# Dividing after the value product: where softmax's reciprocals are multiplied in

## The chip, the cores and the metric

The kernel runs on one core of a Trainium2 chip. The core has five engines that take their instructions in order, each from a queue of its own: TensorE (PE, with its weight loads shown apart as PEld), VectorE (DVE), ScalarE (ACT), GpSimd (POOL) and SyncE (SP), whose queue starts every DMA of this kernel. The metric is the device time of one execution in microseconds; less is better.

## The reference

The program is causal block attention followed by two feed-forward layers:

```python
scores = scale * q @ k.T                      # 4 batches x 8 heads, 576 x 576, head width 64
scores = where(block_i >= block_j, scores, -1e9)   # blocks of 64 positions
attn = exp(scores - max(scores))
attn = attn / (sum(attn) + 1e-09)
x = (attn @ v) as 2304 tokens x 512
x = (x @ w_a) * (x @ w_b) @ w_out             # 512 -> 1536 -> 512
xn = x / rms(x) * rms_g
out = (silu(xn @ w_gate) * (xn @ w_val)) @ w_out2
```

## The kernel before, in words

**Attention.** Two heads go together as a pair `m`; there are 16 pairs, 4 to a batch. A pair's queries are cut into 9 blocks of 64, and for a block `b` both heads' 64 queries stand on the 128 partitions. `score` multiplies block `b` with all its keys (PE, L393, `s` or `mm`), takes the maximum (DVE, L396 to L400, `st`), and writes the exponentials to `pp[b]` (ACT, L402), with their sums beside them. There is one `pp[b]` for each `b`, shared by all pairs. A pair is worked in two parts, blocks 0 to 5 and 6 to 8; a part of a pair is a unit `u`, 32 in all. `p_transposes` turns the probabilities of a unit (PE, L429, to PSUM tile `t`; ACT copies them out, L432), and then the unit is multiplied with the values. For the first 8 pairs that is `whole_values` in plain float32 (PE, L454), whose result, head by head on 64 partitions, is copied to the feed-forward's input `xf` by DVE for the first head and by ACT for the second (L463, the copies at L111 and L109). For the other 8 pairs it is `values`, in two rounded halves (PE, L489), where ACT copies one part out (L494) and DVE adds the other (L495).

**Order.** The loop over `u` works the values of `u - 2`, the transposes of `u - 1` and the scores of `u` in one iteration. The batch of the first 4 pairs runs ahead of the first feed-forward layer; the others are mixed into that layer's matmuls (L597 to L599 for the hidden part, L559 to L561 for the output). A scheduler then fixes every engine's order before the run. All through attention the weights are also decoded and split (`prepare`: L144 and L147 on ACT, L148 and L149 on DVE, L150 on POOL, L109 and L119) and stored to DRAM (L224).

**The DMA queue.** All transfers are started from SP, in order. The input loads of a pair (`kr`, `qz`, `vr`), the weight loads (`ld`, `st`, L187) and the weight stores (`wab`, `wo`, L224) stand in this one queue, and a transfer that waits for its data holds up those behind it.

Of the kernel before, what the change touches and what calls it, by code (L numbers as in the profile page):

```python
# [8 lines left out]
F32 = mybir.dt.float32  # L9
# [4 lines left out]
ALU = mybir.AluOpType  # L14
AX = mybir.AxisListType
PSUM = bass.MemoryType.PSUM
P = 128
# [32 lines left out]
def tile_attention_moe_moe(  # L50
# [13 lines left out]
    pe, act, dve, pool, sp = nc.tensor, nc.scalar, nc.vector, nc.gpsimd, nc.sync  # L64

    B, H, D, S = q.shape
# [23 lines left out]
    dram = ctx.enter_context(tc.tile_pool(name="dram", bufs=1, space=bass.MemoryType.DRAM))  # L90
# [16 lines left out]
    def copy(e, dst, src):  # L107
        if e is act:
            return act.activation(dst, src, AF.Copy)  # L109
        if e is dve:  # L110
            return dve.tensor_copy(dst, src)  # L111
        return pool.tensor_scalar(dst, src, 1.0, 1.0, ALU.mult, ALU.mult)
# [177 lines left out]
    Q = P // 2  # L290
    NQ = S // Q
    PARTS = (range(0, 6), range(6, NQ))
    SCORED = (tuple(PARTS[0]), (NQ - 1, *range(6, NQ - 1)))
    NORM = ({3: (0, 4), 5: (4, 6)}, {NQ - 1: (NQ - 1, NQ), NQ - 2: (6, NQ - 1)})

    def blocks_of(part, j):

        return [b for b in PARTS[part] if b >= 2 * j]
# [8 lines left out]
    def attention(pools, x_of, done):  # L307

        ap, ap2, ps_s, ps_t = pools
        NP = B * H // 2  # L310
        k_raw, v_raw, ks, vv, pt = {}, {}, {}, {}, {}

        st = [ap.tile([P, NQ + 2], F32, name=f"st{x}") for x in range(2)]
        roots = [ap.tile([P, NQ], F32, name=f"rt{x}") for x in range(2)]
# [70 lines left out]
        def score(m, b):  # L385

            nk = Q * (b + 1)
            s, t3, r, pi = st[m % 2], sums[m % 2], roots[m % 2], pp[b]
            halves = [(0, nk)] if nk <= 512 else [(0, nk // 2), (nk // 2, nk)]
            pss = []  # L390
            for a, z in halves:
                ps = ps_s()
                pe.matmul(ps[:, 0:z - a], qz[m % 2][:, b], ks[m][:, a:z], start=True, stop=True)  # L393
                pss.append(ps)
            if len(halves) == 1:
                dve.tensor_reduce(s[:, b:b + 1], pss[0][:, 0:nk], axis=AX.X, op=ALU.max, negate=True)  # L396
            else:
                for x, (a, z) in enumerate(halves):
                    dve.tensor_reduce(s[:, NQ + x:NQ + x + 1], pss[x][:, 0:z - a], axis=AX.X, op=ALU.max)
                dve.tensor_reduce(s[:, b:b + 1], s[:, NQ:NQ + 2], axis=AX.X, op=ALU.max, negate=True)  # L400
            for x, (a, z) in enumerate(halves):
                act.activation(  # L402
                    pi[:, a:z], pss[x][:, 0:z - a], AF.Exp, bias=s[:, b:b + 1], scale=1.0,
                    accum_out=t3[:, b, x:x + 1],
                )
            for norm in NORM:
                if b in norm:
                    b0, b1 = norm[b]
                    t = r[:, b0:b1]
                    dve.tensor_reduce(t, t3[:, b0:b1, :], axis=AX.X, op=ALU.add)  # L410
                    dve.reciprocal(t, t)  # L411
                    for y in range(b0, b1):
                        t = pp[y][:, 0:Q * (y + 1)]
                        pool.tensor_scalar(t, t, r[:, y:y + 1], 1.0, ALU.mult, ALU.mult)  # L414
            return sum(max(107.0, (z - a) / 0.6) for a, z in halves)

        def p_transposes(u):
            m, part = divmod(u, 2)
# [19 lines left out]
        def whole_values(u):  # L438

            m, part = divmod(u, 2)  # L440
            batch, h = divmod(m, H // 2)
            x = x_of(batch)
            b0 = PARTS[part][0]
            src = pt[u][0]
            for g in range(0, len(PARTS[part]), 4):
                bs = list(PARTS[part])[g:g + 4]
                ps = ps_t()
                js = [j for j in range(NTILE) if 2 * j <= bs[-1]]
                cost = 0.0
                for j in js:  # L450
                    first = max(bs[0], 2 * j)
                    at, n = PLACE[part].index((j, first)), (bs[-1] + 1 - first) * P
                    o = (first - bs[0]) * P
                    pe.matmul(  # L454
                        ps[:, o:o + n], vv[m][:, j].rearrange("p h d -> p (h d)"), src[:, at * P:at * P + n],
                        start=(j == 0), stop=(j == js[-1]),
                    )
                    cost += n / 0.6
                cols = slice(bs[0] * Q, (bs[-1] + 1) * Q)
                t = ps[:, 0:len(bs) * P].rearrange("p (n h q) -> p n h q", h=2, q=Q)  # L460
                for hh in range(2):
                    r = slice(hh * D, hh * D + D)
                    copy(dve if hh else act, x[r, h, cols].rearrange("p (n q) -> p n q", q=Q), t[r, :, hh, :])  # L463
                yield cost
            del pt[u]
            if part == 1:
                del vv[m]
                done[batch] = done.get(batch, 0) + 2

        def values(u):  # L470
            m, part = divmod(u, 2)
            batch, h = divmod(m, H // 2)
            x = x_of(batch)
            b0 = PARTS[part][0]
            n = len(PARTS[part]) * Q
            for hh in range(2):
                r, z = slice(hh * D, hh * D + D), slice(D - hh * D, P - hh * D)
                ps = ps_t()
                seq = []
                for j in range(NTILE):  # L480
                    bs = blocks_of(part, j)
                    if bs:
                        at = PLACE[part].index((j, bs[0]))
                        for t in pt[u]:
                            t = t.rearrange("p (n h q) -> p n h q", h=2, q=Q)
                            seq.append((t[:, at:at + len(bs), hh, :], j, (bs[0] - b0) * Q))
                cost = 0.0
                for y, (src, j, o) in enumerate(seq):
                    pe.matmul(  # L489
                        ps[:, o:n], vv[m][:, hh, j, :], src, start=(y == 0), stop=(y == len(seq) - 1)  # L490
                    )
                    cost += (n - o) / 2.4 + 15
                cols = slice(b0 * Q, b0 * Q + n)
                act.activation(x[r, h, cols], ps[z, 0:n], AF.Copy)  # L494
                dve.tensor_tensor(x[r, h, cols], ps[r, 0:n], x[r, h, cols], ALU.add)  # L495
                yield cost
            del pt[u]
            if part == 1:
                del vv[m]
                done[batch] = done.get(batch, 0) + 2  # L500
# [11 lines left out]
        for u in range(2 * NP + 2):  # L512
# [5 lines left out]
            if sc:  # L518
                yield score(m, sc.pop(0))
                if len(sc) > 2:  # L520
                    yield score(m, sc.pop(0))
                if part == 0:
                    make_vv(m)
                else:
                    make_k(m + 1)
            alive = True
            while sc or alive:
                c = next(ct, None) if alive else None
# [346 lines left out]
    n = 0  # L875
# [214 lines left out]
```

## Time and profile before

| | |
|---|---|
| median of 3 runs | 1073.88 us (1072.61 to 1075.56) |
| the profiled execution's own time | 1073.38 us |
| its span, first to last instruction | 1071.6 us |
| PE busy | 1055.9 us of the span |
| DVE, ACT, POOL busy | 708.9, 599.6, 397.0 us |
| POOL, multiplies of `pp` by the reciprocals (L414) | 144 instructions, 87.6 us |

The profile tells for each engine how long it was busy, and for each idle stretch what ended it. The ends of matmuls are modelled and overlap the next one's start, so a busy PE is not PE at its peak. The granted TensorE clock is the full one (1.00) in nearly all of the span.

### The profile page before, as it was taken

What the parts mean: (1) busy time and instruction counts of PE and PEld (TensorE: products, weight loads), DVE (VectorE), ACT (ScalarE), POOL (GpSimd) and SP (SyncE); (2) the same over time, 40 slices, a digit from 0 to 9 for tenths busy, and PEclk for the clock granted to TensorE, in tenths of its full rate; (3) what the DMA queues carried; (4) which work ended last, traced back from release to release, by engine and by line L of the source; (5) the groups of instructions that cost most, each with busy time, mean ns of one, the idle gap of its engine ahead of it and who ended that gap; (6) DMA issues with size and microseconds to landing.
All of it is one profiled execution on the core that took longest, in us unless ns stands there. A gap on an engine that the chain in (4) does not pass through costs nothing.

```text
span 1071.6 us, 16776 instructions
## 1 busy us (share of the span) xinstructions
PE 1055.9 (99%) x5596; PEld 934.0 (87%) x5596; DVE 708.9 (66%) x1339; ACT 599.6 (56%) x1330; POOL 397.0 (37%) x400
## 2 busy tenths in 40 slices
PE   9999999999999999999999999999999999999998
PEld 6767766789998877888887888999999999999998
DVE  6658788556777677545537594692876928657285
ACT  7888776447676666435324542754656546355352
POOL 5747567314456765334314431120221202212020
PEclk9999999999999999999999999999999999999999
DMA  9767875857988888879987988887889888887883
GB/s 242 228 204 242 287 278 203 313 196 250 335 295 286 285 308 294 340 272 343 377 291 302 358 349 308 273 269 253 249 276 325 257 272 250 274 278 233 269 247 118
DMA packets 127772, 295.41 MB, mean 276 GB/s; under 512 B 41155, under 2 KB 53187, under 8 KB 115142
## 3 DMA queue, kind: packets, MB, share of 16 engines
q1 hardware_dynamic: 127686, 294.33, 80.6%
q8 instruction: 45, 0.74, 0.3%
q14 instruction: 41, 0.34, 0.1%
HBM read 232.93 MB, written 61.36 MB: 275 GB/s over the span
## 4 chain that ended last, share of the span: by engine, by line
PE 77%; DMA 2%; POOL 2%; DVE 2%; ACT 1%; issue 1%; POOLq 0%; DVEq 0%; ACTq 0%
PE mm L625 25%; PE mm L656 12%; PE mm L599 7%; PE mm L598 7%; PE mm L597 7%; PE mm L559 3%; PE mm L561 3%; PE mm L560 3%; PE s L393 3%; PE t L489 2%; PE t L429 2%; DMA o<-wo 1%; DMA st<-in_w_ab_dram 1%; POOL src L150 1%; PE t L454 1%
## 5 line engine op out<-in xcount | busy, mean ns | idle before, releaser
L597 PE MATMUL mm<-xh,ab 128*128 128x512 f32 (+1 forms) x480 | 183.1, 384 | 0.0
L599 PE MATMUL mm<-xh,ab 128*128 128x512 f32 (+1 forms) x480 | 181.8, 379 | 0.0
L598 PE MATMUL mm<-xl,ab 128*128 128x512 f32 (+1 forms) x480 | 181.2, 378 | 0.0
L625 PE MATMUL mm<-hT,w 128*128 128x384 f32 x576 | 166.3, 339 | 0.0
L119 POOL TENSOR_TENSOR hl<-g,hh 128x384 fp32r<-128x384 f32 x36 | 42.5, 1180 | 301.3 <-ACT hh L109 292.8
L625 PE MATMUL mm<-hB,w 128*128 128x384 f32 x432 | 127.0, 338 | 0.0
L656 PE MATMUL mm<-hh,w 128*128 128x384 f32 x504 | 125.6, 337 | 0.0
L414 POOL TENSOR_SCALAR pp<-pp,rt 128x64 f32<-128x64 f32 (+3 forms) x144 | 87.6, 623 | 80.8 <-DVE rt L411 48.6
L633 ACT ACTIVATE mm<-mm 128x384 f32<-128x384 f32 x144 | 66.8, 475 | 87.9 <-PE mm L625 49.8
L625 PEld LDWEIGHTS mm<-hT,w 128*128 128x128 f32 x576 | 106.1, 188 | 0.6 <-DVE asb L711 0.2
L597 PEld LDWEIGHTS mm<-xh,ab 128*128 128x128 f32 x480 | 90.4, 188 | 18.1 <-issue 2.8
L598 PEld LDWEIGHTS mm<-xl,ab 128*128 128x128 f32 x480 | 90.4, 188 | 17.2 <-issue 2.6
L599 PEld LDWEIGHTS mm<-xh,ab 128*128 128x128 f32 x480 | 90.4, 188 | 16.8 <-issue 2.0
L625 PE MATMUL mm<-lT,w 128*128 128x384 f32 x288 | 97.5, 338 | 0.0
L393 PE MATMUL s<-ks,qz 128*128 128x64 f32 (+4 forms) x284 | 91.0, 414 | 5.0 <-ACT pp L402 4.8
L402 ACT ACTIVATE pp<-s,st 128x288 f32<-128x288 f32 (+8 forms) x142 | 70.5, 500 | 45.3 <-DVE st L396 35.0
L559 PE MATMUL mm<-hh,o 128*128 128x512 f32 (+1 forms) x240 | 92.3, 386 | 1.1 <-DVE acc L568 1.1
L656 PEld LDWEIGHTS mm<-hh,w 128*128 128x128 f32 x504 | 90.9, 188 | 0.3 <-ACT mm L633 0.3
L560 PE MATMUL mm<-hh,o 128*128 128x512 f32 (+1 forms) x240 | 89.8, 375 | 0.0
L561 PE MATMUL mm<-hl,o 128*128 128x512 f32 (+1 forms) x240 | 88.1, 377 | 0.0
L656 PE MATMUL mm<-hl,w 128*128 128x384 f32 x252 | 81.6, 337 | 0.0
L150 POOL TENSOR_TENSOR src<-src,st 128x512 uint32<-128x512 uint32 x36 | 50.0, 1391 | 82.4 <-DVE st L149 55.9
(140 smaller groups left out, 2333.2 us busy)
## 6 DMA issues: line engine op xcount, KB each, us to landing
w<-wc SPq DMA_DIRECT2D x252, 256.0 KB, 3.6
ab<-wab SPq DMA_DIRECT2D x48, 1024.0 KB, 7.8
w<-wco SPq DMA_DIRECT2D x126, 256.0 KB, 3.5
o<-wo SPq DMA_DIRECT2D x16, 1536.0 KB, 8.5
wc<-bg SPq DMA_DIRECT2D x12, 1792.0 KB, 10.5
st<-in_w_ab_dram SPq DMA_DIRECT2D x34, 512.0 KB, 5.1
wab<-ab SPq DMA_DIRECT2D x12, 1024.0 KB, 4.8
wco<-bg SPq DMA_DIRECT2D x6, 1792.0 KB, 6.8
```

The costliest lines, as they stand in the source:

```text
L393: pe.matmul(ps[:, 0:z - a], qz[m % 2][:, b], ks[m][:, a:z], start=True, stop=True)
L402: act.activation(pi[:, a:z], pss[x][:, 0:z - a], AF.Exp, bias=s[:, b:b + 1], scale=1.0, accum_out=t3[:, b, x:x + 1],)
L414: pool.tensor_scalar(t, t, r[:, y:y + 1], 1.0, ALU.mult, ALU.mult)
L559: pe.matmul(ps[:, 0:n], wh, hh, start=(y == 0), stop=False)
L560: pe.matmul(ps[:, 0:n], wl, hh, start=False, stop=False)
L561: pe.matmul(ps[:, 0:n], wh, hl, start=False, stop=(y == TF - 1))
L597: pe.matmul(ps[:, 0:n], wh[:, a:z], xhc, start=(c == 0), stop=False)
L598: pe.matmul(ps[:, 0:n], wh[:, a:z], xlc, start=False, stop=False)
L599: pe.matmul(ps[:, 0:n], wl[:, a:z], xhc, start=False, stop=(c == KC - 1))
L625: pe.matmul(ps, lhs, rhs[:, c, :], start=(start and c == 0 and y == 0), stop=(c == 1 and y == 2), skip_group_check=not start,)
L633: act.activation(to, ps, AF.Copy)
L656: pe.matmul(banks[m], lhs, rhs, start=(start and f == group[0] and y == 0), stop=(f == group[-1] and y == 2), skip_group_check=not start,)
```

## The change

Before, when all blocks of a group had their sums, DVE added them up and took reciprocals (L410, L411, four groups to a pair), and POOL multiplied every `pp[b]` by its block's reciprocal (L414), before the transposes. Now `pp` stays undivided. DVE forms the reciprocals once for each unit; a DMA writes them as a row to DRAM (`root`), and two DMAs, one for each head, read that row back spread over 64 partitions (`spread`, tile `fa`). `fa` then holds the reciprocal of each query along the free dimension, as the value product has its queries. In `whole_values` the two copies out of PSUM become DVE multiplies by `fa`, for both heads; in `values` a POOL multiply of `xf` by `fa` follows the DVE add.

```diff
-    NORM = ({3: (0, 4), 5: (4, 6)}, {NQ - 1: (NQ - 1, NQ), NQ - 2: (6, NQ - 1)})
...
-            for norm in NORM:
-                if b in norm:
-                    b0, b1 = norm[b]
+            for part in range(2):
+                if b == SCORED[part][-1]:
+                    b0, b1 = PARTS[part][0], PARTS[part][-1] + 1
                     t = r[:, b0:b1]
                     dve.tensor_reduce(t, t3[:, b0:b1, :], axis=AX.X, op=ALU.add)
                     dve.reciprocal(t, t)
-                    for y in range(b0, b1):
-                        t = pp[y][:, 0:Q * (y + 1)]
-                        pool.tensor_scalar(t, t, r[:, y:y + 1], 1.0, ALU.mult, ALU.mult)
+                    row = rows[2 * m + part] = dram.tile([P, b1 - b0], F32, tag=f"root{part}", name="root")
+                    sp.dma_start(out=row, in_=t)
...
+        def spread(u):
+
+            row, n = rows.pop(u), len(PARTS[u % 2])
+            t = factors[u] = ap2.tile([P, Q * n], F32, tag=f"fa{u % 2}", name="fa", bufs=1)
+            for hh in range(2):
+                part = slice(hh * D, hh * D + D)
+                sp.dma_start(out=t[part], in_=row[part].rearrange("q n -> (q n)").partition_broadcast(D))
+
+        def factor(u, r, n0, n1):
+
+            t = factors[u].rearrange("p (q n) -> p n q", q=Q)
+            return t[r, n0 - PARTS[u % 2][0]:n1 - PARTS[u % 2][0], :]
...
-                    copy(dve if hh else act, x[r, h, cols].rearrange("p (n q) -> p n q", q=Q), t[r, :, hh, :])
+                    dve.tensor_tensor(
+                        x[r, h, cols].rearrange("p (n q) -> p n q", q=Q), t[r, :, hh, :],
+                        factor(u, r, bs[0], bs[-1] + 1), ALU.mult,
+                    )
...
+                to = x[r, h, cols].rearrange("p (n q) -> p n q", q=Q)
+                pool.tensor_tensor(to, to, factor(u, r, b0, PARTS[part][-1] + 1), ALU.mult)
...
                 if len(sc) > 2:
                     yield score(m, sc.pop(0))
+                if u > 0:
+                    spread(u - 1)
                 if part == 0:
                     make_vv(m)
                 else:
                     make_k(m + 1)
+            elif u == 2 * NP:
+                spread(u - 1)
```

In the orders below, line numbers of the changed kernel are its own: its L392, L395 and L398 are the scores and maxima of L393, L396 and L399 before, its L440 the transposes of L429, and its L409, L410, L412, L421 and L474 are the sum, the reciprocal, the row's write, its two reads and the multiply.

On DVE, early in the first batch, where the first unit's value product is taken out of PSUM (`rt_140`, `st_138`: sums and maxima of the second pair; `st_137`: of the third). Before:

```order
L148 TENSOR_SCALAR x<-a 128x512
L410 TENSOR_REDUCE rt_140<-su_142 128x4
L411 RECIPROCAL rt_140<-rt_140 128x4
L111 COPY xf<-t 64x256
L410 TENSOR_REDUCE rt_140<-su_142 128x2
L396 TENSOR_REDUCE st_138<-mm 128x1
```

Now:

```order
L398 TENSOR_REDUCE st_138<-s 128x1
L409 TENSOR_REDUCE rt_140<-su_142 128x6
L395 TENSOR_REDUCE st_137<-mm 128x1
L474 TENSOR_TENSOR xf<-t,fa 64x256
L474 TENSOR_TENSOR xf<-t,fa 64x128
L474 TENSOR_TENSOR xf<-t,fa 64x256
L474 TENSOR_TENSOR xf<-t,fa 64x128
L395 TENSOR_REDUCE st_138<-s 128x1
L399 TENSOR_REDUCE st_138<-st_138 128x1
L410 RECIPROCAL rt_140<-rt_140 128x6
```

Four multiplies stand together later in the queue than the first copy did, and the next maxima and the second pair's reciprocals stand behind them.

On SP's queue, from the first weight load on (`rt_139`: reciprocals of the first pair). Before:

```order
L187 DMA ld<-in_w_ab_dram 128x512 x2
L341 DMA kr<-in_k_dram 128x576
L347 DMA qz_149<-in_q_dram 64x9x64 x2
L359 DMA vr<-in_v_dram 128x5x64 x2
L187 DMA ld<-in_w_ab_dram 128x512
```

Now:

```order
L187 DMA ld<-in_w_ab_dram 128x512
L412 DMA root<-rt_139 128x6
L187 DMA ld<-in_w_ab_dram 128x512
L340 DMA kr<-in_k_dram 128x576
L346 DMA qz_149<-in_q_dram 64x9x64 x2
L358 DMA vr<-in_v_dram 128x5x64 x2
L421 DMA fa<-root 64x384 x2
L412 DMA root<-rt_139 128x3
L187 DMA ld<-in_w_ab_dram 128x512
```

The row's write comes between two weight loads, and its reads come six loads later.

On PE, in the first pair, where its transposes begin (`pp_155` to `pp_158` are its blocks 0 to 3). Before:

```order
L393 MATMUL s<-ks,qz_149 128x320
L393 MATMUL mm<-ks,qz_149 128x288
L393 MATMUL s<-ks,qz_149 128x288
L393 MATMUL mm<-ks,qz_149 128x512
L393 MATMUL mm<-ks,qz_150 128x128
L429 MATMUL t<-ident,pp_155 128x128
```

Now:

```order
L392 MATMUL s<-ks,qz_149 128x320
L440 MATMUL t<-ident,pp_155 128x128
L392 MATMUL mm<-ks,qz_149 128x288
L440 MATMUL t<-ident,pp_156 128x128
L392 MATMUL s<-ks,qz_149 128x288
L440 MATMUL t<-ident,pp_157 128x128
L440 MATMUL t<-ident,pp_158 128x128
```

The first transposes stand four scores earlier.

## Rows read from the trace of the kernel before

**Rows 1.** The page: span, and busy time of each engine over it.

```profile
span 1071.6 us, 16776 instructions
...
PE 1055.9 (99%) x5596; PEld 934.0 (87%) x5596; DVE 708.9 (66%) x1339; ACT 599.6 (56%) x1330; POOL 397.0 (37%) x400
```

**Rows 2.** Windows: length, then busy of PE, PEld, DVE, ACT, POOL; clock, DMA, GB/s.

```profile
0.00:90.00 90.00, 86.22 (x402) 64.01 (x403) 61.03 (x154) 73.05 (x198) 55.96 (x81) 1.00 0.77 221
90.00:200.00 110.00, 103.56 (x460) 77.59 (x459) 87.17 (x154) 79.70 (x180) 70.70 (x63) 1.00 0.75 266
200.00:450.00 250.00, 249.20 (x1509) 214.09 (x1508) 169.99 (x395) 153.55 (x383) 124.38 (x144) 1.00 0.81 286
450.00:660.00 210.00, 208.75 (x922) 172.69 (x921) 123.64 (x177) 83.47 (x135) 74.32 (x56) 1.00 0.85 324
660.00:1072.00 412.00, 408.16 (x2311) 405.58 (x2309) 267.02 (x462) 209.78 (x434) 71.62 (x58) 1.00 0.81 259
```

**Rows 3.** Waits of PE, 0 to 200 us: total us, times, longest.

```profile
PE s L393 <- ACT pp L402: 4.8, 6, 2.0
...
PE mm L393 <- ACT pp L402: 0.7, 1, 0.7
...
PE t L429 <- POOL pp L414: 0.5, 1, 0.5
...
PE mm L393 <- POOL pp L414: 0.2, 1, 0.2
```

**Rows 4.** Waits of the weight loads, 0 to 200 us.

```profile
PEld s L393 <- ACT pp L402: 8.8, 13, 2.3
...
PEld t L429 <- POOL pp L414: 1.6, 5, 0.7
```

**Rows 5.** Lines: operation, tile, shape, count, busy us, mean ns.

```profile
L414 POOL TENSOR_SCALAR pp<-pp,rt 128x64 f32<-128x64 f32 (+3 forms) x144 | 87.6, 623 | 80.8 <-DVE rt L411 48.6 <-ACT ph L432 6.7 <-ACT asb L602 6.2
...
L234 POOL TENSOR_TENSOR src<-src 128x256 f32<-128x256 f32 x18 | 15.7, 871 | 1.0
...
L411 DVE RECIPROCAL rt<-rt 128x4 f32<-128x4 f32 (+2 forms) x64 | 10.6, 165 | 1.6
...
L410 DVE TENSOR_REDUCE rt<-su 128x4 f32<-128x12 f32 (+2 forms) x64 | 9.9, 155 | 18.4 <-ACT pp L402 18.0
...
L111 DVE COPY xf<-t 64x256 f32<-64x256 f32 (+2 forms) x24 | 8.6, 361 | 7.1 <-ACT xf L109 6.5
...
L109 ACT ACTIVATE xf<-t 64x256 f32<-64x256 f32 (+2 forms) x24 | 7.7, 323 | 3.5 <-PE t L454 3.5
```

**Rows 6.** Lines by form, the same columns.

```profile
L495 DVE TENSOR_TENSOR xf<-t,xf 64x384 f32<-64x384 f32 x16 | 8.9, 554 | 2.1 <-ACT xf L494 1.8
...
L495 DVE TENSOR_TENSOR xf<-t,xf 64x192 f32<-64x192 f32 x16 | 5.7, 354 | 5.5 <-ACT xf L494 5.1
```

**Rows 7.** Windows: length, busy of L414 on POOL alone, clock, DMA, GB/s.

```profile
0.00:200.00 200.00, 46.10 (x71) 1.00 0.76 246
```

**Rows 8.** DMA issues, 10 to 17 us: count, KB each, median us to landing.

```profile
ld<-in_w_ab_dram SPq DMA_DIRECT2D x3, 512.0 KB, 5.9
vr<-in_v_dram SPq DMA_DIRECT2D x2, 160.0 KB, 7.1
```

**Rows 9.** Timeline of the DMA queue (SPq), from 13 us.

```profile
12.98 3.25 SPq L359 DMA_DIRECT2D vr<-in_v_dram  x2
16.27 1.59 SPq L187 DMA_DIRECT2D ld<-in_w_ab_dram  x1
```

**Rows 10.** Timeline of DVE, at 23 us.

```profile
23.37 0.27 DVE L396 TENSOR_REDUCE st<-mm 128x1 f32<-128x128 f32 x1
```

**Rows 11.** Timeline of the DMA queue (SPq), at 65 us.

```profile
64.77 0.33 SPq L187 DMA_DIRECT2D ld<-in_w_ab_dram  x1
```

**Rows 12.** Timeline of DVE, at 73 us.

```profile
73.46 0.42 DVE L111 CAST xh<-xf 128x512 fp32r<-128x512 f32 x1
```

**Rows 13.** DMA issues of the whole span, a small row read back from DRAM.

```profile
sm<-row SPq DMA_DIRECT2D x3, 3.0 KB, 2.8
```

More of the change, by code (lines that the diff above doesn't have):

```diff
@@ L310, in attention @@
         NP = B * H // 2
-        k_raw, v_raw, ks, vv, pt = {}, {}, {}, {}, {}
+        k_raw, v_raw, ks, vv, pt, rows, factors = {}, {}, {}, {}, {}, {}, {}
         st = [ap.tile([P, NQ + 2], F32, name=f"st{x}") for x in range(2)]
@@ L462, in whole_values @@
                     r = slice(hh * D, hh * D + D)
-                    copy(dve if hh else act, x[r, h, cols].rearrange("p (n q) -> p n q", q=Q), t[r, :, hh, :])
+                    dve.tensor_tensor(
+                        x[r, h, cols].rearrange("p (n q) -> p n q", q=Q), t[r, :, hh, :],
+                        factor(u, r, bs[0], bs[-1] + 1), ALU.mult,
+                    )
                 yield cost
-            del pt[u]
+            del pt[u], factors[u]
             if part == 1:
@@ L495, in values @@
                 dve.tensor_tensor(x[r, h, cols], ps[r, 0:n], x[r, h, cols], ALU.add)
+                to = x[r, h, cols].rearrange("p (n q) -> p n q", q=Q)
+                pool.tensor_tensor(to, to, factor(u, r, b0, PARTS[part][-1] + 1), ALU.mult)
                 yield cost
-            del pt[u]
+            del pt[u], factors[u]
             if part == 1:
```

## The prediction

> **What bounds the kernel now.** First the page: PE is busy 1055.9 of the span's 1071.6 us [rows 1], so all that any change off PE can give back is 15.7 us of idle PE, and a little of what the modelled ends of matmuls hide. Then the stages [rows 2], to see where those 15.7 us lie. PE's busy time is short of the stretch by 3.8 us in 0 to 90 us (batch 0, attention nearly alone), by 6.4 us in 90 to 200, by 0.8 us in 200 to 450, where the other half of attention runs, and by 1.3 and 3.4 us in the two stages after it (the span ends at 1071.6). So two thirds of the idle PE time, 10.2 us, are in the first 200 us, where DVE is busy 148 us, ACT 153 and POOL 127. Behind 450 us the change leaves everything alone.
>
> Then PE's waits in those 200 us [rows 3]: scores that wait for ACT's exponentials to free their PSUM tile, 4.8 + 0.7 = 5.5 us, and 0.5 + 0.2 = 0.7 us that POOL's multiplies end. The weight loads stand nearer to the real stall, since their ends are not stretched [rows 4]: 8.8 us for the exponentials, 1.6 us for POOL. The multiplies that the change removes are thus seldom what PE waits for in person.
>
> **What it removes.** All 144 POOL multiplies, 87.6 us at 623 ns [rows 5]; 71 of them, 46.1 us, are recorded in the first 200 us [rows 7], which takes POOL there from 127 to 81 us. Of ACT it takes the 24 copies of `xf`, 7.7 us at 323 ns [rows 5], 5% of ACT's 153 us. Of DVE it takes two of the four sums and reciprocals of a pair, 32 of each: 32 x (0.155 + 0.165) = 10.2 us [rows 5], half of it in the first 8 pairs.
>
> What this gives on PE: the 0.7 us that POOL ends go for certain, and up to the 1.6 us that the weight loads show; I take 1.2. For the waits on exponentials, ACT's queue is 5% shorter and the probabilities of a block are transposed as soon as they are written, so `pp` is free earlier for the next pair; I take half of the 5.5 us, 2.7, and half a microsecond for the stalls between. That is 4.4 us gained. The bounds: nothing, if the waits only change their name, and 9 us, nearly all of the 10.2.
>
> **What it adds in work.** In the first 8 pairs DVE does 48 multiplies out of PSUM instead of 24 copies. The nearest row is L495, also PSUM with SBUF on 64 partitions: 554 ns for 384 columns and 354 for 192 [rows 6], so 1.04 ns a column over 154 ns. A 64x256 multiply is then 420 ns, a 64x128 287, a 64x192 354, and a pair takes 2 x (420 + 287 + 354) = 2.12 us. Eight pairs take 17.0 us against 8.6 us of copies [rows 5]. With the 5.1 us of sums and reciprocals gone, DVE's first 200 us grow by 3.3 us on 148. DVE has 52 us free there; I put it at nothing, and at 3.3 us if every one fell on the path. In the last 8 pairs POOL gets 32 multiplies of 64x384 and 64x192. Taking L234's 871 ns for 256 columns [rows 5] as the middle, that is 28 us in place of 41.5 us, on a POOL that is busy 124 of 250 us [rows 2]. They come behind the PSUM tile's release, and only the split of the next block needs them: nothing.
>
> **What it adds in waits.** SP issues 32 writes and 64 reads more. An issue took 0.33 us where the queue was quiet [rows 11] and 1.6 us where it was crowded [rows 9], so 96 of them are 32 to 154 us of SP's time, spread over the 450 us of attention; SP computes nothing, and I put the issues by themselves at nothing. What can cost is that a factor is late, because in the first 8 pairs the multiply that waits for it stands in DVE's queue, in front of maxima that PE's PSUM tiles wait for.
>
> Take unit 0. Its reciprocals were ready at about 10 us. On SP its reads stand behind the `vr` loads, whose second ended its issue at 16.2 us [rows 9]; with the row's own issue added the reads leave at about 16.7 and 17.2 us. What was issued there took 5.9 to 7.1 us to land [rows 8], so the factors are there at 22.6 to 24.3 us. On DVE the multiplies stand behind the maximum that ran from 23.37 to 23.64 us [rows 10]. On the old clock that is late by at most 0.7 us; but a DVE that gets there two microseconds sooner waits those two, and the early gain is gone. Unit 7, the last of batch 0: its reads stand behind the weight load issued at 64.8 us [rows 11], so they land at about 71 us, and the multiply stands before the rounding of `xf` for the first feed-forward block, which ran at 73.46 us [rows 12]. That one is in time, by 2 us. Going so through the order of the 16 units of the first 8 pairs I count five (an estimate: it sets the new order beside old times) where read and multiply stand within about a microsecond of each other. At half a microsecond each that is 2.5 us of DVE, and I let all of it reach PE. The bounds: 0, and 16 us if all 16 are late by a microsecond. In the last 8 pairs the multiply waits on POOL, where weight decoding is behind it, with a unit to every 250 / 16 = 15.6 us; I put that at nothing, and at 1 us if one decode is late.
>
> The Trainium skill has a rule that would make these hops shorter (DMA: Bandwidth & Descriptors, Latency and other measured facts): a DMA's fixed cost is about 2 us, mostly the write receipt from HBM, and rises with HBM's load. By it write and read would take about 4 us, unit 0's factors would land near 19 us, and the 2.5 us would be 0. The trace disagrees for this stretch: 5.9 to 7.1 us there [rows 8]; a 3 KB row read back later took 2.8 us in the median [rows 13]. The measurement decides.
>
> **The sum.** 1073.4 us is the profiled execution's own time (span 1071.6), half a microsecond below the median. 1073.4 - 4.4 + 2.5 = 1071.5 us, 2.4 us or 0.2% under the median.
>
> **The rivals.** A difference of up to 0.3%, 3.2 us, cannot be told from no change here; so "same" is 1070.7 to 1077.1 us.
>
> (a) My forecast, about the same: the relief on POOL and ACT and the late factors nearly cancel, or POOL's relief reaches PE in nothing at all, since the exponentials, not the multiplies, end most of the waits [rows 3, 4]. 1068.5 to 1076 us, chance 0.41.
>
> (b) The factors are in time: the sum without the 2.5 us, and more of the 10.2 idle microseconds given back. For it: 46 us less on POOL and 8 on ACT in exactly the stage with the idle PE. Against it: DVE is as full as before. 1073.4 - 7.5 = about 1066 us, between 1064.4 (all 9 us) and 1070. Chance 0.34. The 2 us of the Trainium skill's page on DMA, cited above, would make this the case.
>
> (c) Slower, by one mechanism: multiplies at the head of DVE's queue that wait for `fa` in most of the 16 units. If they are late by x us each on average, the time is 1073.4 - 4.4 + 16x. It gets slower than the bound where 16x is over 8, that is x over 0.5 us; at 0.75 us it is 1081 us. For it: the DMA queue is busy 0.75 to 0.77 of the time in this stage [rows 2], each row goes through it twice, and every read waits on SP for the write to land, with weight loads behind. Against it: a unit's scores, transposes and values are spread over three iterations. Chance 0.25.
>
> **How the numbers follow.** Faster (b) 0.35, same (a) 0.39, slower (c) 0.26, with a little of (a) given to both neighbours. The range goes from 1065, most of (b), to 1080, half of (c). For (a) alone it is 1068.5 to 1076.
>
> **What would show it.** Right: L414 gone; POOL near 81 us in the first 200; the new DVE multiplies at 290 to 420 ns; PE idle there down from 10.2 to about 8 us; DVE waits on the `fa` DMAs of some 2 to 3 us, in a few units, unit 0 among them. For (b): no such wait, and PE idle under 5 us. For (c): waits of DVE on `fa` of 8 us or more, with PE waiting for maxima or exponentials behind them. I am wrong in kind if the time moves behind 450 us, or if PE loses time between 200 and 450 us.

## The result, and the profile after

The changed kernel takes 1087.14 us in the median of 5 runs (1084.74 to 1089.36), against 1073.88 before: a ratio of 1.0118, with a 95% interval of 1.0096 to 1.0140. It is slower by 12.7 us, and outside the range that was given. Differences below are such ratios, each against runs of the kernel before on the same chip, times its 1073.9 us; intervals reach 1 to 2.5 us to either side, 3.3 us for one kernel (`queue_pool`). The profiled execution of the changed kernel took 1089.36 us, the longest of the five.

The page of the changed kernel, answering to [rows 1], and its count of packets (before: 127772 packets, 295.41 MB):

```profile
span 1087.2 us, 16662 instructions
...
PE 1064.1 (98%) x5596; PEld 937.4 (86%) x5596; DVE 715.0 (66%) x1299; ACT 596.1 (55%) x1306; POOL 339.3 (31%) x288
...
DMA packets 137499, 300.20 MB, mean 276 GB/s; under 512 B 46787, under 2 KB 62915, under 8 KB 124870
```

POOL has lost 58 us of work, as meant, and the DMA queue has gained 4.8 MB, 1.6%, in 9700 small packets. The windows by stage, with the columns of [rows 2], and then four shorter stretches:

```profile
0.00:90.00 90.00, 81.37 (x355) 57.66 (x355) 53.41 (x130) 62.60 (x168) 23.34 (x32) 0.94 0.82 216
90.00:200.00 110.00, 106.03 (x471) 81.34 (x470) 94.27 (x151) 81.09 (x176) 56.67 (x40) 0.98 0.81 258
200.00:450.00 250.00, 245.01 (x1461) 208.57 (x1461) 165.93 (x354) 148.26 (x372) 104.72 (x95) 1.00 0.88 291
450.00:660.00 210.00, 207.99 (x937) 171.35 (x936) 127.58 (x194) 88.61 (x149) 79.12 (x62) 1.00 0.87 327
```

```profile
20.00:30.00 10.00, 8.07 (x39) 5.31 (x39) 7.83 (x18) 7.02 (x19) 4.23 (x4) 1.00 0.88 244
30.00:40.00 10.00, 6.69 (x16) 3.59 (x15) 4.46 (x10) 6.50 (x19) 3.24 (x4) 0.71 1.09 248
40.00:50.00 10.00, 8.50 (x34) 5.50 (x33) 6.60 (x18) 6.77 (x17) 0.00 (x0) 0.84 0.84 281
50.00:60.00 10.00, 10.00 (x44) 7.08 (x43) 4.94 (x12) 6.78 (x21) 4.74 (x4) 0.93 0.73 153
```

Read the first table for where PE's busy time went. In 0 to 90 us it is 4.9 us less than in [rows 2], in 200 to 450 us 4.2 us less; only 90 to 200 has gained, by 2.5 us. The second table shows that the first stage is worse than its idle time: with PE busy only 8.07 and then 6.69 of 10 us, the granted clock goes to 0.71, 0.84 and 0.93, a mixture of the two levels of 1.2 and 2.4 GHz, where before it was 1.00 in these stretches. Busy time at such a clock does less work: (1 - 0.71) x 6.69 + (1 - 0.84) x 8.50 + (1 - 0.93) x 10.0 = 4.0 us, an estimate. DMA's share in 200 to 450 us has risen from 0.81 to 0.88.

What happened there is seen in the timelines of SP's queue, of DVE and of PE (start, length, engine, line; in brackets the idle time before, and what ended it):

```profile
13.56 2.95 SPq L358 DMA_DIRECT2D vr<-in_v_dram  x2
16.61 2.38 SPq L421 DMA_DIRECT2D fa<-root  x2
19.09 0.53 SPq L412 DMA_DIRECT2D root<-rt  x1
...
22.74 1.19 SPq L421 DMA_DIRECT2D fa<-root  x2
```

```profile
23.22 0.28 DVE L395 TENSOR_REDUCE st<-mm 128x1 f32<-128x128 f32 x1
23.42 1.80 DVE L474 TENSOR_TENSOR xf<-t,fa 64x256 f32<-64x256 f32 x4
...
30.49 0.48 DVE L395 TENSOR_REDUCE st<-s 128x1 f32<-128x64 f32 x2
34.02 0.83 DVE L474 TENSOR_TENSOR xf<-t,fa 64x192 f32<-64x192 f32 x2 [3.05 <-DMA fa<-root]
```

```profile
34.95 2.04 PE L465 MATMUL t<-pw,vr 128*128 128x512 f32 x2 [3.31 <-issue]
```

Unit 0's multiplies, at 23.42 us, wait for nothing. Unit 1's are late, for two reasons. The `vr` loads and the two reads of unit 0 kept SP until 18.99 us, so unit 1's row, whose reciprocals were ready at 14.55 us, left at 19.09, and its reads at 22.74 to 23.93. And these reads took 11.1 us to land, where the median of their kind is 4.3: from 19 to 34 us the DMA engines were full, now and before the change, and loads landed after 9.5 to 12.2 us now, after 4.2 to 9.1 before. Now (first the time of the queue's packets as a share of the 16 engines' time):

```profile
q1 hardware_dynamic: 2692, 3.76, 94.4%
...
fa<-root SPq DMA_DIRECT2D x2, 48.0 KB, 11.1
```

Before, with the slowest of the loads:

```profile
q1 hardware_dynamic: 3795, 4.47, 101.9%
...
qz<-in_q_dram SPq DMA_DIRECT2D x2, 144.0 KB, 9.1
```

With a landing of 7.1 us, the longest that the prediction reckoned with, unit 1's factors would have been there at 30.3 us, before DVE stopped at 30.97. So DVE stood 3.05 us before the multiply of 34.02. PE's next value product came 0.1 us behind that multiply's end, after 3.31 us of nothing, and then the clock had fallen. The profile names no releaser for this wait of PE ("issue"); that it was the multiply is read from the times. The waits of PE and of DVE in 0 to 200 us, answering to [rows 3] (us in total, times, longest):

```profile
PE t L465 <- issue: 3.3, 1, 3.3
PE mm L579 <- ACT hh L109: 2.6, 1, 2.6
PE s L392 <- ACT pp L401: 1.4, 4, 0.6
...
PE mm L392 <- ACT pp L401: 0.8, 1, 0.8
```

```profile
DVE xf L474 <- DMA fa<-root: 5.8, 5, 3.0
```

The waits for exponentials that were 4.8 + 0.7 us are now 1.4 + 0.8: the relief came, and was spent elsewhere. The new multiplies, by form, with the columns of [rows 6]:

```profile
L511 POOL TENSOR_TENSOR xf<-xf,fa 64x384 f32<-64x384 f32 x16 | 19.6, 1224 | 45.9 <-DMA fa<-root 36.5 <-DVE xf L509 7.2 <-ACT xf L508 1.6
L511 POOL TENSOR_TENSOR xf<-xf,fa 64x192 f32<-64x192 f32 x16 | 10.5, 656 | 15.5 <-DVE st L149 5.4 <-DMA fa<-root 4.8 <-DVE xf L509 3.9
L474 DVE TENSOR_TENSOR xf<-t,fa 64x256 f32<-64x256 f32 x16 | 10.0, 626 | 5.0 <-DMA fa<-root 4.7
L474 DVE TENSOR_TENSOR xf<-t,fa 64x192 f32<-64x192 f32 x16 | 6.5, 404 | 12.7 <-PE t L465 7.8 <-DMA fa<-root 4.6
L474 DVE TENSOR_TENSOR xf<-t,fa 64x128 f32<-64x128 f32 x16 | 6.1, 380 | 0.4 <-PE t L465 0.3
```

The transfers of the trip (count, KB each, median us from issue to landing), and SP's wait between them:

```profile
fa<-root SPq DMA_DIRECT2D x32, 96.0 KB, 4.7
fa<-root SPq DMA_DIRECT2D x32, 48.0 KB, 4.3
root<-rt SPq DMA_DIRECT2D x16, 3.0 KB, 5.8
root<-rt SPq DMA_DIRECT2D x16, 1.5 KB, 7.3
```

```profile
SPq L421 <- DMA root<-rt: 95.6, 26, 7.7
```

### The profile page after: what moved, and what is told of

It reads as the page before. It is cut to its first block, busy times and chain, and to the rows that moved or that the text cites. A ratio compares the mean times of both kernels' runs of the same rounds, so it can differ in the third digit from the quotient of the medians.

```text
span 1087.2 us, 16662 instructions
## 1 busy us (share of the span) xinstructions
PE 1064.1 (98%) x5596; PEld 937.4 (86%) x5596; DVE 715.0 (66%) x1299; ACT 596.1 (55%) x1306; POOL 339.3 (31%) x288
## 4 chain that ended last, share of the span: by engine, by line
PE 66%; DMA 6%; POOL 6%; issue 5%; DVE 3%; ACT 3%; SPq 0%; POOLq 0%; DVEq 0%; ACTq 0%
PE mm L645 25%; PE mm L676 12%; PE mm L617 5%; PE mm L618 5%; PE mm L619 5%; PE mm L579 3%; PE mm L580 3%; PE mm L581 3%; DMA st<-in_w_ab_dram 2%; PE s L392 2%; DMA root<-rt 2%; POOL src L150 1%; POOL x L150 1%; DMA wc<-bg 1%; PE t L503 1%
## 5 line engine op out<-in xcount | busy, mean ns | idle before, releaser
L392 PE MATMUL s<-ks,qz 128*128 128x64 f32 (+4 forms) x284 | 93.0, 417 | 3.6 <-ACT pp L401 3.6
L645 PEld LDWEIGHTS mm<-hB,w 128*128 128x128 f32 x432 | 79.8, 188 | 0.1
```

The lines of the kernel that those rows point to most:

```text
L645: pe.matmul(ps, lhs, rhs[:, c, :], start=(start and c == 0 and y == 0), stop=(c == 1 and y == 2), skip_group_check=not start,)
```

## The experiments

Three theories were tried. A: the trip through DRAM costs, either by factors that come late (A1) or by its transfers in SP's queue (A2). B: the moved arithmetic and the new order cost. Several kernels multiply by a constant tile of ones, so that no factor can be late; their result stays undivided.

**Arithmetic without the trip, and the trip without its use.** `no_dma` drops the writes and reads; `unused_dma` keeps them all and does not use what they bring.

```diff
+        flat = [ap2.tile([P, Q * len(PARTS[x])], F32, ...) for x in range(2)]   # 1.0, both kernels
-            t = factors[u].rearrange("p (q n) -> p n q", q=Q)
+            t = flat[u % 2].rearrange("p (q n) -> p n q", q=Q)
-                    sp.dma_start(out=row, in_=t)      # no_dma alone, and its spread()
```

> The change without its DMAs: no row is written or read back, and the multiplies use tiles that hold 1.0 from the start, so the result is left undivided. Theory A (the trip through DRAM costs it: factors come late, and SP's queue is held while a read waits for its row): the loss goes, and what the relief on POOL and ACT is worth shows, 1064 to 1071 us; PE busy in the first 90 us back to 86 us or more, granted clock 1.00 there. Theory B (the moved arithmetic and the new order of the instructions cost it, the DMAs are hidden): still 1080 us or more.

> All DMAs of the change stay, but the multiplies use tiles that hold 1.0, so that nothing waits for a factor (the result is left undivided). Theory A1 (the multiplies that wait on DVE and POOL for a late factor): about as fast as the run without DMAs, within 3 us of it. Theory A2 (SP's queue, held by reads that wait for their row, with input and weight loads behind them): about as slow as the changed kernel, 1082 to 1089 us. Theory B: 1080 us or more too, and then the run without DMAs is as slow.

`no_dma`: 1068.35 us, ratio 0.9947 (0.9928 to 0.9965), 5.7 us faster than before. `unused_dma`: 1080.7 us, 1.0055 (1.0037 to 1.0074), 5.9 us slower. So B falls: the arithmetic is a gain. `unused_dma` lies between the cases of A1 and A2, and both have their part: the transfers alone cost 11.6 us (A2), and waiting for the factors the other 6.8 us of the change (A1).

**Half the pairs.** The change for the first 8 pairs alone, or the last 8, the others as before:

```diff
-            for part in range(2):
+            if m // (H // 2) < WHOLE:      # first_half;  >= WHOLE: second_half
```

> The change for the first 8 pairs alone; the last 8 are divided on POOL as before. By the trace, matmuls of the first feed-forward block are 11 us late at 44 us and some 9 us late from 200 to 430 us, and 15.5 us late from 467 us on. If the two losses are separate: 1083 to 1086 us here. If the second loss (the end of attention) is what counts and the first is made up again: under 1078 us.

> The change for the last 8 pairs alone; the first 8 are divided on POOL as before. If the two losses are separate: 1077 to 1080 us, with the whole loss of 3 to 6 us between 340 and 470 us. If POOL's wait for late factors there costs nothing on PE: 1072 to 1075 us.

`first_half` 1079.7 us, 1.0066 (1.0043 to 1.0088); `second_half` 1077.81 us, 1.0042 (1.0025 to 1.0059). Each half costs, 7.1 and 4.5 us, together 11.6 of the whole change's 12.7. `second_half` is what was expected of two separate losses; `first_half` lies between its two cases.

**Is it the held queue?** H says that reads which wait for their row hold up what stands behind them in SP's queue, N that the transfers cost by being there. First `no_hold` (reads of a constant DRAM row), 1080.67 us, whose start came late because that row had to be written ahead of the first loads; then `reads_input` without this flaw. In both, no read waits for its row.

```diff
-    sp.dma_start(out=t[part], in_=row[part].rearrange("q n -> (q n)").partition_broadcast(D))
+    sp.dma_start(out=t[part], in_=k[0, 0][0:1, 0:Q * n].rearrange("q n -> (q n)").partition_broadcast(D))
```

> As unused_dma (all 96 transfers are issued, the multiplies take a constant tile, so the result is undivided), but the reads take a constant DRAM row that was written once at the start: no read stands in the queue until its own row has landed, and each lands in the same places as before. It tells what of the 12.4 us between no_dma (1068.4) and unused_dma (1080.7) is the holding of the queue, and what the 96 transfers themselves. Theory H (a read that waits for its row holds the weight loads and stores behind it): 1068 to 1072 us, and the queue's wait for root, 93.0 us in unused_dma, is gone. Rival N (96 more issues of 1 to 1.5 us and their small packets on a crowded queue): 1079 to 1082 us, although that wait is gone. Between: both, in that proportion.

> As no_hold, without its flaw: there a DRAM row had to be written first, ahead of the first loads, and the start of the kernel came 2 to 5 us later. Here the 64 reads take a row of an input, which needs nothing written; the 32 row writes stay, and the multiplies take a constant tile, so the result is undivided. Theory H (the held reads cost the 12.4 us between 1068.4 and 1080.7): 1068 to 1072 us. Theory N (the 96 transfers cost by being there, held or not): 1078 to 1082 us, with the loss at the end of attention (430 to 460 us) still there.

`reads_input`: 1079.66 us, 1.0055 (1.0038 to 1.0071), the same time as `unused_dma`, as N says. But the two lose it in different places (0 to 200 and 200 to 450 us, columns as in [rows 2]), `reads_input` first, then `unused_dma`:

```profile
0.00:200.00 200.00, 187.71 (x846) 141.13 (x847) 147.27 (x290) 144.83 (x350) 81.85 (x74) 0.98 0.90 263
200.00:450.00 250.00, 247.84 (x1484) 211.68 (x1483) 173.42 (x364) 152.67 (x381) 110.88 (x99) 1.00 0.83 284
```

```profile
0.00:200.00 200.00, 191.42 (x870) 141.94 (x871) 156.80 (x296) 149.16 (x359) 82.82 (x74) 1.00 0.84 261
200.00:450.00 250.00, 242.36 (x1453) 207.91 (x1452) 166.69 (x357) 148.65 (x371) 112.08 (x99) 0.99 0.87 286
```

With no row to wait for, the reads also moved: the fixed order has all 64 of them in the first 150 us (in `no_hold` in the first 157), where `unused_dma` has them spread over 459 us. SP still stood 25.2 us before reads of `reads_input`, until an earlier read into the same tile had landed, and the loss that was expected from 430 to 460 us is small there (PE busy 29.41 us, against 26.39). So the equal times do not clear the held queue by themselves. `narrow_reads`, below, does: it keeps the held reads, 85.4 us of them against 93.0 in `unused_dma`, and is 7.8 us faster. My favourite, H, falls: the holding is worth about nothing.

**Other queues.** The same transfers started by POOL or by ACT (`sp.dma_start` becomes `pool.` or `act.dma_start` in both places). POOL's own queue moved their 4.80 MB in 3584 packets, where SP's took some 9700.

> The changed kernel whole, but the row writes and reads are started by POOL, whose queue has no other transfers and which is busy only a third of the time. Theory H (SP's queue is held up for its weight transfers): the 12.4 us of the queue are saved, and the factors land earlier since they stand behind no weight load, so most of the 6.4 us of late factors too: 1068 to 1074 us. Rival N (the transfers themselves, wherever they are started): 1080 to 1087. Rival P (POOL, which now waits for each row between its issue and the reads, holds up the weight decoding behind it): no faster than 1080 either, with POOL's waits for root of 50 us or more and PE stalls behind it.

> The changed kernel whole, but the row writes and reads are started by ACT. SP is as free as with queue_pool, but ACT's exponentials, for whose PSUM tiles PE waits most often, stand behind each read that waits for its row. If a wait costs by what stands behind it: ACT waits for root for some 50 to 100 us in all, and the time is well above the 1087 us of the change, 1095 to 1130. If the transfers themselves cost, wherever they are started: 1085 to 1090.

`queue_pool`: 1092.3 us, 1.0168 (1.0138 to 1.0199). `queue_act`: 1113.65 us, 1.0361 (1.0338 to 1.0384). Neither helps, as N and P say: the transfers stay, and now an engine with work stands before them. POOL's wait in `queue_pool`:

```profile
POOL fa L421 <- DMA root<-rt: 51.7, 16, 8.0
```

For ACT I expected 50 to 100 us of visible waits for `root`; the trace names only 6 us so, and puts some 35 us of idle ACT down to issue, so that its loss is measured but its split is not. The Trainium skill (DMA: Bandwidth & Descriptors, Issuing engines are not separate DMA queues) says that transfers started on different engines run on the same 16 DMA engines, and that spreading them saves only the time to start them; that neither run gained agrees with it.

**What in the transfers?** `writes_only` has no reads; `narrow_reads` fills 1 partition of 64; `quarter_reads` 16 of 64; `short_reads` a quarter of each row in all 64; `own_rows` reads 64 different rows of an input instead of one. All multiply by ones.

```diff
-    sp.dma_start(out=t[part], in_=row[part].rearrange("q n -> (q n)").partition_broadcast(D))
+    sp.dma_start(out=t[hh * D:hh * D + 1], in_=...partition_broadcast(1))               # narrow_reads
+    sp.dma_start(out=t[hh * D:hh * D + D // 4], in_=...partition_broadcast(D // 4))     # quarter_reads
+    sp.dma_start(out=t[part, 0:D * n // 4], in_=row[hh * D:hh * D + D // 4]...)         # short_reads
+    sp.dma_start(out=t[part], in_=k[0, 0][0:D, 0:Q * n])                                # own_rows
```

> As unused_dma, with the 32 row writes alone and none of the 64 reads; result undivided. The writes wait on SP for DVE's reciprocals (29.8 us in the changed kernel) but for no transfer. If what costs goes by the number of transfers, a third of 12.4 us: about 1072.5. If it is the reads (their waits or their bytes): about 1069. If it is the writes' wait on DVE: 1078 or more.

> As unused_dma (held reads, multiplies by a constant tile, result undivided), but each read fills one partition instead of 64: the 96 issues and their waits stay, 4.7 MB and some 4000 packets go. If issues and holding cost: about 1080 us, as unused_dma. If the bytes and packets of the spreading cost, on DMA queues that are busy 0.75 to 0.85 of the time: 1068 to 1073 us.

> As unused_dma (1080.7 us, result undivided), each read still fills 64 partitions but only a quarter of their elements: all 4096 packets, a quarter of the bytes (1.2 of 4.7 MB). If packets cost: about 1080. If bytes cost: 1072 (narrow_reads) plus a quarter of the 8.7 us between, about 1074.

> As unused_dma (result undivided), each read fills 16 partitions instead of 64, whole rows: a quarter of the packets and a quarter of the bytes. By either of the two about 1074; with own_rows and short_reads it tells whether the cost falls in proportion (1074) or only when nearly all is gone (1077 or more).

> As reads_input (1079.7 us), but each of the 64 partitions reads a row of its own of the input, where before all 64 read one and the same 1.5 KB (0.8 KB for the small part). Same number of transfers, packets and bytes. If the one row that all packets of a read share is what is slow: 1070 to 1073 us. If it is the bytes and packets: 1078 to 1081.

| kernel | read, MB | packets of reads | median us | ratio (interval) | against before |
|---|---|---|---|---|---|
| no_dma | 0 | 0 | 1068.35 | 0.9947 (0.9928 to 0.9965) | -5.7 |
| writes_only | 0 | 0 | 1070.13 | 0.9971 (0.9957 to 0.9984) | -3.1 |
| narrow_reads | 0.07 | 64 | 1072.0 | 0.9982 (0.9970 to 0.9994) | -1.9 |
| quarter_reads | 1.2 | 1024 | 1073.79 | 1.0002 (0.9988 to 1.0015) | +0.2 |
| short_reads | 1.2 | 4096 | 1074.82 | 1.0004 (0.9995 to 1.0014) | +0.4 |
| own_rows | 4.7 | 4096 | 1076.89 | 1.0028 (1.0016 to 1.0040) | +3.0 |
| unused_dma | 4.7 | 4096 | 1080.7 | 1.0055 (1.0037 to 1.0074) | +5.9 |

From `narrow_reads` to `unused_dma` the number of reads is the same, and SP's waits for their rows are alike (82 to 93 us); what the reads carry grows, and with it the time. `own_rows` is apart: it has the early reads of `reads_input` and the same order as that kernel on PE and SP, and is to be set beside it. A quarter of the bytes costs 2.1 us with a quarter of the packets and 2.3 with all of them, of 7.8 us in all: it goes by bytes and not by packets, and in proportion as far as intervals of 1 to 2 us can tell. That all read one row may be some 3 us of it: `own_rows`, between its two cases, lies below `reads_input`, but the intervals touch. In 0 to 460 us (length; busy PE, PEld, DVE, ACT, POOL; clock, DMA, GB/s), `no_dma`, `narrow_reads` and `unused_dma`:

```profile
0.00:460.00 460.00, 454.38 (x2442) 370.38 (x2443) 333.40 (x672) 306.14 (x750) 199.48 (x181) 1.00 0.80 273
```

```profile
0.00:460.00 460.00, 451.51 (x2426) 366.69 (x2427) 329.48 (x668) 303.36 (x742) 194.71 (x177) 1.00 0.82 270
```

```profile
0.00:460.00 460.00, 443.78 (x2374) 358.26 (x2375) 327.28 (x660) 301.46 (x737) 194.90 (x173) 1.00 0.86 274
```

From the second to the third PE loses 7.7 us of busy time, close to the 7.8 of the ratios (these two executions themselves lie 10.7 us apart), and DMA's share rises from 0.82 to 0.86. The held reads are there in `narrow_reads` too, as SP's wait in its first 470 us shows:

```profile
SPq L425 <- DMA root<-rt: 85.4, 27, 5.7
```

What PE waits for can be followed at one stall of `unused_dma`. ACT stood 4.00 us for a weight load, the next exponentials stood behind its decoding, and PE stood 1.99 us for them:

```profile
427.89 0.66 ACT L144 ACTIVATE st<-st 128x512 uint32<-128x512 uint32 x1 [4.00 <-DMA st<-in_w_o_dram]
...
430.86 0.52 ACT L405 ACTIVATE pp<-s,st 128x320 f32<-128x320 f32 x1
```

```profile
431.53 0.75 PE L396 MATMUL s<-ks,qz 128*128 128x288 f32 x2 [1.99 <-ACT pp L405]
```

From 200 to 470 us ACT stood 20.8 us for weight loads in `unused_dma` and 10.3 in `narrow_reads`. In `no_dma`, without any trip, it was 14.0, so late weight loads are a hint of the way, and not shown to be all of it.

The fixed orders differ between such kernels, since the scheduler sees the transfers: `unused_dma` and `narrow_reads` have another PE instruction (by operation and tiles) in 489 of 5596 places. PE's order alone is not the cause, since `reads_input` and `narrow_reads` differ in only 157 and lie 7.8 us apart as well. The orders of the other queues differ more, and no run holds them fixed, so that a part of the 7.8 us may be theirs.

**Copy first, multiply later.** For the first 8 pairs the PSUM tile is copied out as before the change (by ACT for the first head and by DVE for the second, as the code has it), without a wait, and POOL multiplies in place:

```diff
-                    dve.tensor_tensor(..., t[r, :, hh, :], factor(u, r, bs[0], bs[-1] + 1), ALU.mult)
+                    to = x[r, h, cols].rearrange("p (n q) -> p n q", q=Q)
+                    copy(dve if hh else act, to, t[r, :, hh, :])
+                    pool.tensor_tensor(to, to, factor(u, r, bs[0], bs[-1] + 1), ALU.mult)
```

> The changed kernel with its transfers in SP's queue, but in the first 8 pairs the PSUM tile is copied out by DVE and ACT as before the change, without waiting for a factor, and POOL multiplies the result in place afterwards, as the last 8 pairs already do. It tells whether the 6.4 us between the change (1087.1) and unused_dma (1080.7) are multiplies at the head of DVE's queue. If they are: 1079 to 1083 us, the first 60 us without the stall of 3.3 us before the value product and with the granted clock near 1.00 there. If the factors' lateness holds the feed-forward's input itself, whoever multiplies: 1085 to 1090.

1082.32 us, 1.0082 (1.0060 to 1.0105): 3.9 of the 6.8 us of A1 come back, and PE is busy 9.45 of 10 us from 30 to 40 us in place of 6.69. So more than half of A1 goes with the multiplies at the head of DVE's queue, though the intervals of the two ratios (1.0096 to 1.0140 and 1.0060 to 1.0105) touch. The clock there was 0.83, better than 0.71 and not the 1.00 that I expected.

**Without DRAM.** The factors can be made on DVE: it transposes the reciprocals, repeated along the free dimension, in blocks of 32 x 32, and POOL copies the blocks that belong to the other half of a head's partitions. `dve_spread` does this for the first 8 pairs and leaves the last 8 as before the change; `dve_spread_all` does it for all 16.

```diff
-            for hh in range(2):
-                sp.dma_start(out=t[part], in_=row[part]...partition_broadcast(D))
+            t = factors[u] = ap2.tile([P, n, 2, D // 2], F32, tag=f"fa{u % 2}", name="fa")
+            dve.transpose(t.rearrange("p n a q -> p n (a q)"), row.unsqueeze(2).to_broadcast([P, n, D]))
+            for a in range(0, P, D):
+                i, j = slice(a, a + D // 2), slice(a + D // 2, a + D)
+                copy(pool, t[i, :, 1, :], t[j, :, 1, :])
+                copy(pool, t[j, :, 0, :], t[i, :, 0, :])
```

> The change without any transfer, for the first 8 pairs: DVE transposes the reciprocals, repeated along the free dimension, in blocks of 32 by 32 into fa, and POOL copies the four blocks that belong to the other half of the partitions; multiplies out of PSUM on DVE as in the change. The last 8 pairs divide the probabilities as before. If the DRAM trip is all that the change loses by, this keeps most of the 5.7 us that no_dma showed, less some 8 us of transposes on DVE that is not the bound: 1068 to 1071 us, faster than both kernels. If more work on DVE reaches PE in the first 200 us: 1072 to 1076.

> As dve_spread (1070.3 us), but for all 16 pairs: the factors are made on DVE and POOL without a transfer, and in the last 8 pairs POOL multiplies xf afterwards as in the change. If the last 8 pairs' arithmetic is worth something too, as no_dma (1068.4) hints: 1068 to 1070 us. If DVE's transposes in 200 to 450 us, where PE has no idle time, only add work: 1071 to 1074.

`dve_spread`: 1070.29 us in the median of 7 runs, 0.9963 (0.9950 to 0.9976), faster than both kernels, by 4.0 us than before. `dve_spread_all`: 1076.43 us, 1.0026 (1.0015 to 1.0037), slower than either case that was expected. In 200 to 450 us, where PE had 0.8 us to win, it loses 4.8:

```profile
200.00:450.00 250.00, 244.44 (x1480) 211.08 (x1479) 181.16 (x376) 151.44 (x376) 128.97 (x163) 0.99 0.79 279
```

`no_dma` has the same multiplies with no factors to make, and PE is busy 249.44 us there, which points to the making of the factors. The lines of `dve_spread`:

```profile
L112 POOL TENSOR_SCALAR fa<-fa 32x192 f32<-32x192 f32 x32 | 12.6, 393 | 15.9 <-DVE fa L432 14.2
...
L489 DVE TENSOR_TENSOR xf<-t,fa 64x256 f32<-64x256 f32 x16 | 6.7, 418 | 1.1 <-PE t L480 0.9
L489 DVE TENSOR_TENSOR xf<-t,fa 64x192 f32<-64x192 f32 x16 | 5.6, 350 | 2.8 <-PE t L480 2.7
L432 DVE STREAM_TRANSPOSE fa<-rt 128x384 f32<-128x384 f32 x8 | 4.6, 576 | 0.2
L489 DVE TENSOR_TENSOR xf<-t,fa 64x128 f32<-64x128 f32 x16 | 4.5, 284 | 0.4 <-PE t L480 0.3
```

**The layout of the factors, and reads into half of the partitions.** The multiplies are faster here than in the change, since these factors lie one behind the other; a DMA row has them 24 or 12 bytes apart. `no_dma_dense` is `no_dma` with the dense layout. `both_heads` is `unused_dma` with one read into 128 partitions in place of two into 64.

```diff
-            t = flat[u % 2].rearrange("p (q n) -> p n q", q=Q)
+            t = flat[u % 2].rearrange("p (n q) -> p n q", q=Q)                # no_dma_dense
+            both = row.rearrange("(h q) n -> h (q n)", h=2).unsqueeze(1)      # both_heads
+            sp.dma_start(out=t, in_=both.to_broadcast([2, D, Q * n]))         # both_heads
```

> As no_dma (1068.4 us, result undivided), with the constant factors laid out one after the other as the multiply reads them, where the change's layout has 24 or 12 bytes from one to the next. The multiplies on DVE should fall from 622, 380 and 403 ns to about 418, 284 and 351, as in dve_spread: 5 us less on DVE. If DVE is near the path in the first 200 us: 1064 to 1066. If it has slack there: 1067 to 1069.

> As unused_dma (1080.7 us, result undivided), but one read for both heads into all 128 partitions in place of two into 64 each: 64 transfers in place of 96, the same 4.7 MB and packets. If the bytes cost wherever they land: 1078 to 1080 (32 issues fewer are worth some 1 us). If a read into half of the partitions is what is slow, since it reaches half of SBUF's ports (the Trainium skill, SBUF — State Buffer, section Door 1: The DMA port swizzle, says so): well under that, 1072 to 1076.

`no_dma_dense`: 1066.65 us, 0.9924 (0.9903 to 0.9946); the multiplies took 420, 286 and 351 ns. It looks 2.5 us better than `no_dma`, but the intervals overlap. `both_heads`: 1111.46 us, 1.0341 (1.0318 to 1.0364), far worse than either case that I had thought of, and no answer to the question of the ports. In the trace's packet records the 128 packets of one of its larger reads ran about two at a time and took 4.4 to 6.6 us in the first 470 us; in `unused_dma`, where two reads bring the same 128, up to 18 ran at once, in 1.6 to 3.8 us. The Trainium skill (DMA: Bandwidth & Descriptors, Rules for kernel authors) has a rule for it: an outermost dimension of size c, where c is below 16, confines a DMA to at most c engines. This read's source begins with a 2, and the two packets at a time agree.

## Why the prediction was wrong

The arithmetic of the sum held better than its price for the trip. Point by point:

- **The gain of 4.4 us.** Right in kind and place: with no trip it is 5.7 us. POOL in the first 200 us is 23.34 + 56.67 = 80.0 us, for 81 forecast, and PE's waits for exponentials fell from 5.5 to about 2.2 us.
- **The multiplies.** 420, 287 and 354 ns were forecast, and are what `dve_spread` measured; the change itself has 626, 380 and 404, in all 22.6 us for 17.0. I read L495's price, whose operands lie dense [rows 6], for an operand that does not. Mis-sized; its weight on the time, some 2.5 us, is not certain.
- **Late factors, 2.5 us.** They cost 6.8 (the change against `unused_dma`). I named the wrong unit: unit 0 waits for nothing, unit 1 waits 3.05 us. The reads of unit 0 hold SP for 2.4 us in front of unit 1's row, and unit 1's reads land after 11.1 us and not 5.9 to 7.1: I took one landing time, from 10 to 17 us [rows 8], for every unit. I also let a microsecond of DVE be a microsecond of PE, but the granted clock fell behind the idle time, and by the estimate above that cost about 4 us more.
- **"SP computes nothing, and I put the issues by themselves at nothing."** This is the step that failed. The transfers cost 11.6 us with no factor waited for: 2.6 for the writes, 1.2 for the reads as such, and 7.8 for the bytes that a spread row becomes. The first two, which are the issues and their waits, are no larger than the intervals, so that putting them at nothing was not far off. The sum had no term for bytes, with [rows 2] showing a DMA queue that was 0.75 to 0.81 busy; 4.7 MB at the mean 276 GB/s is 17 us of that queue.
- **The last 8 pairs, "nothing", or 1 us.** `second_half` costs 4.5 us. The POOL multiplies' wait for `fa` (41.3 us) is there; the runs do not tell how much of the 4.5 is that wait and how much the bytes.
- **The rivals.** (c) had the sign and a true mechanism, multiplies waiting at the head of DVE's queue, yet its 5.8 us of waits lie below the 8 us that it asked for; most of the loss came by another way. "I am wrong in kind if PE loses time between 200 and 450 us" is what happened: 249.20 us became 245.01.
- **The rule on 2 us.** From issue to landing, with any wait behind other transfers, a write and a read took 5.8 and 4.7 us in the median, 7.3 and 4.3 for the small part. Even the 3 KB row is far above 2 us, so the trace disagrees with the Trainium skill's fixed cost (DMA: Bandwidth & Descriptors, Latency and other measured facts) over attention as a whole.

By the runs the sum is -5.7 + 2.6 + 1.2 + 7.8 + 6.8 = +12.7 us; each term is the step from one kernel to the next, so that they must add up, and the sum is no proof of them. By which transfers the bytes reach PE stays open: one stall was followed to a weight load, which is a hint and no more. A second stall of 2.0 us in `unused_dma`, for a hidden block at 438.64 us, was not followed to a transfer. It also stays open whether landing in 64 partitions at a time makes these bytes dearer.

## What to carry to other kernels

On a DMA queue that is already 0.8 busy, price a new transfer by its bytes after spreading (here 1.7 us per MB), and only then by its issue; a 3 KB row that becomes 192 KB is not small. A landing time read in one stretch does not hold for the next: it was 5.9 to 7.1 us at 10 to 17 us before the change, and 11.1 us from 23 us on in the changed kernel, with the DMA engines full. The division done last gained 4.0 us here, with the factors made on the chip and for the first 8 pairs alone, where PE had idle time; for all 16 it lost. A multiply that waits for a transfer does not belong at the head of a queue that PE waits for.

## What was not expected of the hardware

- One idle stretch of 3.3 us of PE, with PE busy 8.07 of 10 us before it, was followed by granted clocks of 0.71, 0.84 and 0.93 in three stretches of 10 us. In `copy_then_pool`, without such a stall, 7.38 of 10 us and then 9.45 went with 1.00 and then 0.83.
- A DVE multiply of 64x256 out of PSUM took 418 ns with dense f32 factors and 626 with one every 24 bytes; 64x192 took 350, and 404 with one every 12 bytes. POOL's 64x384 in SBUF took 1035 ns dense (`no_dma_dense`) and 1224 to 1272 spaced. The Trainium skill (SBUF — State Buffer, Door 1: The DMA port swizzle) has SBUF read in lines of 16 bytes, where each access that crosses to a new line pays; the rows agree in that the wider spacing pays more.
- 32 DMAs whose sources begin with a dimension of 2 cost the kernel 31 us more than 64 whose sources begin with 64 (`both_heads` against `unused_dma`).
- DVE's transpose of 128x384 in blocks of 32 x 32 out of a repeated operand took 576 ns, 128x192 374 to 376 ns.
